# Attention's transposes as pairs of 64-row tiles, and where the early weights are converted

## The chip, the cores and the metric

One core of a Trainium2 chip runs the whole program in one launch. The metric is the device time of a run in microseconds (us); a kernel's figure is the median of its runs. TensorE is PE in the profile (PEld are its weight loads), VectorE is DVE, ScalarE is ACT, GpSimd is POOL, SyncE is SP.

## The reference, cut to what matters

```
# q, k, v: (2, 12, 448, 64); causal softmax attention, heads side by side -> x (896, 768)
scores = q k^T / 8, masked above the diagonal
attn = exp(scores - max) / (sum + 1e-9);  x = attn v
# first product pair: w_in (768, 2048), w_out (2048, 768), alpha (2048)
h = x @ w_in;  g = max(h, 0) + alpha * min(h, 0);  x = g @ w_out
# second: w1, w2, w3, w_out2, all (768, 768)
h = max(x @ w1, x @ w2, x @ w3);  out = h @ w_out2
```

## The kernel before, in words

**Products.** The weights arrive as 64-bit floats, two 32-bit words each. `Weights` turns one 128-column tile (six blocks of 128x128, 768 columns in all) into a high and a low 32-bit part, wh and wl; activations are split the same way (xh, xl or g_h, g_l). A product is three matmuls, xh wh + xl wh + xh wl (`product`, L463). Converting one tile takes these steps: a load (`raw`, L414), on ScalarE `size` (t, L426) and `low` (r, L444), on VectorE two fast operations in `high` (L430, L433), then `top` (L447) and `both` (L458, an integer addition), then wh (a cast on ScalarE, L318) and wl (a subtraction, L330).

**Attention.** There are 12 jobs, numbered 0 to 11, each a pair of heads. Keys run forwards for the first head of the pair and backwards for the second. The 448 queries form four chunks c = 0 to 3 of 64, 128, 128 and 128 rows, which see 64, 192, 320 and 448 keys. For each job:

- scores (L645) on TensorE, as pairs of 64-row matmuls, one per head, in groups of chunks (3, 0) and (2, 1); each group takes two banks of PSUM of a ring "s" of four. The 64x64 scores of chunk 0 stand first in their group;
- a masked row maximum on VectorE (L663), an exp on ScalarE (L676), one reciprocal step per group on VectorE (L688 adds eps, L689), and the normalizing of each part on GpSimd (L693), all in place in a tile e;
- 16 transposes of 128x128 on TensorE (L720, L717), four to a bank of a ring "t" of three, and four copies p of up to 512 columns out of PSUM, on ScalarE (L318) or VectorE (L324);
- the sums with v on TensorE (`pv`, L735), a cast to xh on ScalarE (L318) and xl on VectorE (L330).

**What sets the order.** All this is issued in one order per engine that a planner (`Plan`) writes before the run: of the steps that can start, it takes the one that starts earliest by its own assumed durations, and among nearly equal ones that with the lowest rank. Each engine then runs its list strictly in that order. Job i has rank 10 i plus a number per kind of step (`RANK`). Scores run two jobs ahead of the sums. `port` marks steps of VectorE that the planner keeps apart from GpSimd's.

**Early tiles.** The first three tiles of w_in (f = 0, 1, 2) are held: they are converted while attention runs, with rank 125 + 5 f - 7, and TensorE multiplies them with the first 384 tokens (the first batch) between the last jobs: 54 products of 384 columns. After attention come their 512 other tokens, then the remaining 13 tiles, then w_out, then the second pair of products. The fourth tile (f = 3) starts with a product of 384 columns.

Of the kernel before, what the change touches and what calls it, by code (L numbers as in the profile page):

```python
# [32 lines left out]
    norm=6, p=7, p_out=-4, av=6, x=15, weights=-7, prelu=-10,  # L33
# [169 lines left out]
def attention_moe_moe2_kernel(  # L203
# [25 lines left out]
    B, HP, _, _, S = qk.shape  # L229
    D = 64  # L230
    DM, NT = out.shape
    DFF = alpha.shape[0] * alpha.shape[1]
# [105 lines left out]
    class Weights:  # L338
# [3 lines left out]
        def __init__(  # L342
# [7 lines left out]
            lo_engines=("DVE", "POOL"),  # L350
            after=(),
            token="ct",
            used=None,
        ):
# [13 lines left out]
            size = plan.add(  # L368
                rank, on_act(k, words=True), partial(self.size), (load,), take=(token,)
            )  # L370
            self.size_step = size
            high = plan.add(
                rank, {"DVE": 2 * on_dve(k, fast=True)["DVE"] + 0.12}, step(self.high), (size,), port=True
            )
            low = plan.add(
                rank, on_act(k, words=True), step(self.low), (load,), take=("cr",)
            )
            top = plan.add(
                rank, on_dve(k), step(self.top), (high, low), give=(("raw", load),), port=True
            )  # L380
            both = plan.add(
                rank, on_dve(k) | on_pool(k), self.both, (top, low), give=(("cr", low),), port=True
            )
            self.whole = both
            used = used or slice(0, n)
            k = (used.stop - used.start) * P
            hi = plan.add(
                rank,
                on_act(k),
                copy(lambda: self.part(0)[:, : used.stop - used.start], lambda: f32(self.t[:, used])),  # L390
                (both,),
            )
            lo = plan.add(
                rank,
                {e: (on_dve(k) | on_pool(k))[e] for e in lo_engines},
                sub(
                    lambda: self.part(1)[:, : used.stop - used.start],
                    lambda: f32(self.t[:, used]),
                    lambda: self.part(0)[:, : used.stop - used.start],
                ),  # L400
                (hi,),
                give=((token, size),) if used.stop - used.start == n and token == "ct" else (),
                port=True,
            )
            self.ready = [lo]
# [15 lines left out]
        def size(self, engine):  # L421
            if self.token == "ct":
                self.t = wcvt.tile([P, KC, P], U32, tag="t", name="t")[:, : self.n]
            else:
                self.t = room[self.token].tile([P, KC, P], U32, tag="t", name="t")[:, : self.n]
            nc.scalar.activation(out=f32(self.t), in_=f32(self.raw[..., 1]), func=AF.Abs)  # L426

        def high(self):
            t = self.t
# [12 lines left out]
        def low(self):  # L442
            self.r = wcvt.tile([P, KC, P], U32, tag="r", name="r")[:, : self.n]
            nc.scalar.activation(out=self.r, in_=self.raw[..., 0], func=AF.Copy, scale=2.0**-29)  # L444

        def top(self):
            nc.vector.scalar_tensor_tensor(  # L447
                out=self.t,
                in0=self.raw[..., 1],
                scalar=0xC0000000,  # L450
                in1=self.t,
                op0=ALU.bitwise_and,
                op1=ALU.bitwise_or,
            )

        def both(self, engine):
            t = self.t.bitcast(I32)
            ENGINE[engine].tensor_tensor(out=t, in0=t, in1=self.r.bitcast(I32), op=ALU.add)  # L458
# [1017 lines left out]
```

## Time and profile before

| | |
|---|---|
| median of three runs | 488.33 us (488.0 to 488.43) |
| the profiled execution | 488.39 us, of which the span is 486.6 us |
| TensorE busy | 480.6 us, 99% of the span |
| VectorE, ScalarE, GpSimd busy | 384.0 (79%), 250.3 (51%), 53.7 us (11%) |
| chain that ended last, by engine | PE 88%, DVE 6%, ACT 5%, issue 1% |
| granted TensorE clock | full in all 40 slices |
| HBM | 119 GB/s over the span |

Attention lies in the first 90 us. The span is shorter than the execution, since it runs from the first to the last instruction that the profile shows. Matmuls overlap, so starts, not lengths, give TensorE's pace; on the other engines too an instruction's length includes a tail of some 0.1 us that lies beside the next one.

### The profile page before, as it was taken

How to read it: one execution, taken by the hardware profiler on the slowest of the kernel's cores; microseconds unless marked ns; L12 is line 12 of the kernel's file. 1: busy time of each engine (PE TensorE's matmuls, PEld its weight loads, DVE VectorE, ACT ScalarE, POOL GpSimd, SP SyncE). 2: the span in 40 equal slices, each digit the busy share in tenths (PEclk: the TensorE clock that was granted, in tenths of full speed). 3: DMA queues.
4: the chain of work that ended last, by engine and by line, in shares of the span. 5: the costliest groups of instructions: out<-in, count | busy, mean ns of one | idle time of the engine just before them, and what ended most of it. 6: DMA issues, size and time to landing. Idle time of an engine off the chain costs nothing.

```text
span 486.6 us, 7335 instructions
## 1 busy us (share of the span) xinstructions
PE 480.6 (99%) x2727; PEld 415.6 (85%) x2727; DVE 384.0 (79%) x750; ACT 250.3 (51%) x478; POOL 53.7 (11%) x101
## 2 busy tenths in 40 slices
PE   9999999999999999999999999999999999999997
PEld 4766668889888999898898899988899988899986
DVE  5789988589999999866647557589899999716962
ACT  5899996145535544534344425365455665305510
POOL 4557675010000000000000000000000000000000
PEclk9999999999999999999999999999999999999999
DMA  7666511113323332425233333344433554000122
GB/s 275 241 205 210 195 49 67 65 66 129 118 88 120 130 116 67 137 95 164 61 120 114 113 120 129 101 159 151 166 139 129 201 188 131 0 1 1 57 96 75
DMA packets 13859, 58.28 MB, mean 120 GB/s; under 512 B 1664, under 2 KB 3328, under 8 KB 13824
## 3 DMA queue, kind: packets, MB, share of 16 engines
q1 hardware_dynamic: 13680, 57.72, 35.5%
q8 instruction: 21, 0.34, 0.3%
q14 instruction: 14, 0.11, 0.1%
q10 hardware_dynamic: 144, 0.10, 0.1%
HBM read 55.06 MB, written 2.75 MB: 119 GB/s over the span
## 4 chain that ended last, share of the span: by engine, by line
PE 88%; DVE 6%; ACT 5%; issue 1%; POOL 0%; DVEq 0%; ACTq 0%
PE ps L463 79%; PE ps L645 3%; ACT e L676 3%; PE pv L735 3%; PE pt L720 3%; DVE xl L330 1%; DVE e L663 1%; ACT p L318 1%; PE warm L801 1%; DVE wl L330 1%; DVE t L958 1%; PE pt L717 0%; ACT xh L318 0%; DVE v L1141 0%; ACT wh L318 0%
## 5 line engine op out<-in xcount | busy, mean ns | idle before, releaser
L463 PE MATMUL ps<-xh,wl 128*128 128x384 f32 (+2 forms) x435 | 158.0, 363 | 0.0
L463 PE MATMUL ps<-xh,wh 128*128 128x384 f32 (+2 forms) x435 | 157.9, 363 | 0.0
L463 PE MATMUL ps<-xl,wh 128*128 128x384 f32 (+2 forms) x435 | 157.8, 363 | 0.0
L463 PEld LDWEIGHTS ps<-xh,wh 128*128 128x128 f32 x435 | 81.7, 188 | 8.8
L463 PEld LDWEIGHTS ps<-xl,wh 128*128 128x128 f32 x435 | 81.6, 188 | 8.7
L463 PEld LDWEIGHTS ps<-xh,wl 128*128 128x128 f32 x435 | 81.7, 188 | 8.5
L318 ACT CAST wh<-t 128x768 fp32r<-128x768 f32 (+1 forms) x52 | 42.2, 811 | 68.7 <-DVE t L458 68.5
L463 PE MATMUL ps<-g_h,wl 128*128 128x512 f32 (+1 forms) x192 | 69.7, 363 | 0.0
L463 PE MATMUL ps<-g_l,wh 128*128 128x512 f32 (+1 forms) x192 | 69.6, 363 | 0.0
L463 PE MATMUL ps<-g_h,wh 128*128 128x512 f32 (+1 forms) x192 | 69.5, 362 | 0.0
L330 DVE TENSOR_TENSOR wl<-t,wh 128x768 fp32r<-128x768 f32 (+1 forms) x48 | 44.2, 921 | 17.6 <-ACT wh L318 17.6
L458 DVE CUSTOM_DVE_ANT_0 t<-t,r 128x1536 uint16<-128x1536 uint16 (+1 forms) x58 | 53.6, 926 | 2.0
L447 DVE SCALAR_TENSOR_TENSOR t<-raw,t 128x768 uint32<-128x768 uint32 (+1 forms) x58 | 53.6, 925 | 0.9
L444 ACT ACTIVATE r<-raw 128x768 uint32<-128x768 uint32 (+1 forms) x58 | 50.9, 878 | 6.4 <-DMA raw<-in_moe_w_dram 4.5
L426 ACT ACTIVATE t<-raw 128x768 f32<-128x768 f32 (+1 forms) x58 | 51.1, 883 | 5.7 <-DMA raw<-in_moe_w_dram 3.2
L693 POOL TENSOR_SCALAR e<-e,sm 128x192 f32<-128x192 f32 (+3 forms) x84 | 43.7, 538 | 30.4 <-DVE sm L689 16.8
L676 ACT ACTIVATE e<-e,nm 128x192 f32<-128x192 f32 (+3 forms) x84 | 43.8, 526 | 5.8 <-DVE nm L663 5.6
L318 ACT CAST g_h<-g 128x384 fp32r<-128x384 f32 (+1 forms) x32 | 18.2, 568 | 49.4 <-DVE g L773 49.3
L463 PEld LDWEIGHTS ps<-g_l,wh 128*128 128x128 f32 x192 | 36.0, 188 | 3.9
L463 PEld LDWEIGHTS ps<-g_h,wh 128*128 128x128 f32 x192 | 36.1, 188 | 3.9
L463 PEld LDWEIGHTS ps<-g_h,wl 128*128 128x128 f32 x192 | 36.0, 188 | 3.8
L663 DVE CUSTOM_DVE_ANT_0 e<-ps,mask 128x192 f32<-128x192 f32 (+2 forms) x72 | 32.0, 486 | 8.8 <-PE ps L645 8.6
(95 smaller groups left out, 526.7 us busy)
## 6 DMA issues: line engine op xcount, KB each, us to landing
raw<-in_moe_w_dram SPq DMA_DIRECT2D x18, 768.0 KB, 4.3
raw<-in_moe_w_in_dram SPq DMA_DIRECT2D x16, 768.0 KB, 4.4
raw<-in_moe_w_out_dram SPq DMA_DIRECT2D x12, 768.0 KB, 4.4
raw<-in_moe_w_out_dram SPq DMA_DIRECT2D x12, 640.0 KB, 4.1
qk<-in_qk_dram SPq DMA_DIRECT2D x12, 448.0 KB, 3.6
v<-in_v_dram SPq DMA_DIRECT2D x12, 448.0 KB, 4.3
out_dram<-o SPq DMA_DIRECT2D x11, 224.0 KB, 1.9
out_dram<-o SPq DMA_DIRECT2D x1, 128.0 KB, 1.7
```

Of the source, the lines that this page charges most:

```text
L318: nc.scalar.copy(out(), src())
L330: ENGINE[engine].tensor_tensor(out=out(), in0=a(), in1=f32(b()), op=ALU.subtract)
L426: nc.scalar.activation(out=f32(self.t), in_=f32(self.raw[..., 1]), func=AF.Abs)
L444: nc.scalar.activation(out=self.r, in_=self.raw[..., 0], func=AF.Copy, scale=2.0**-29)
L447: nc.vector.scalar_tensor_tensor(out=self.t, in0=self.raw[..., 1], scalar=0xC0000000, in1=self.t, op0=ALU.bitwise_and, op1=ALU.bitwise_or,)
L458: ENGINE[engine].tensor_tensor(out=t, in0=t, in1=self.r.bitcast(I32), op=ALU.add)
L463: nc.tensor.matmul(ps, a, c, start=(first and y == 0), stop=(last and y == 2), **kw)
L645: nc.tensor.matmul(ps if c else ps[rows * j : rows * j + rows], self.qk[d, 0, START[c] : START[c] + rows], self.qk[d, 1, S - n :] if j els ...
L663: nc.vector.tensor_tensor_reduce(out=self.e_part(c, j), in0=self.ps[c, j], in1=masks[j][:, m : m + n] if c else short, op0=ALU.add, op1=AL ...
L676: nc.scalar.activation(out=s, in_=s, func=AF.Exp, scale=-1.0, bias=self.column(self.nm, i, c, j), accum_out=self.column(self.sm, i, c, j),)
L693: ENGINE[engine].tensor_scalar(out=s, in0=s, scalar1=self.column(self.sm, i, c, j), scalar2=1.0, op0=ALU.mult, op1=ALU.mult,)
L720: nc.tensor.transpose(pt[:, o : o + P], self.e[:, s : s + P], ident)
```

## The change

**Transposes.** A job's 16 transposes become 32 of 64 rows (64 rows of e, 128 columns; 64 columns out). Two that follow each other take the upper and the lower 64 rows and write different banks. They are issued in two phases of 16: the first needs only chunks 2 and 3 normalized and takes two banks of "t", the second takes one bank of "t" and a borrowed one: the next free bank of the scores' ring "s", or for the last two jobs a bank of the later products ("b"). Four copies of 512 columns bring them out, in strips of 64 columns.

**Scores.** The groups are (3), (2, 1); chunk 0 moves out of them: `first` computes it after the sums of the job two before, as a 128x64 pair (q for it comes from the host padded with zeros, so the q/k transfer grows from 448 to 480 KB). Its result lies in columns 448 to 511 of the first bank of group (3), which thus comes free only after the 64-column maximum; that bank is the one that the next second phase borrows.

**Weights of the early tiles.** Each step handles half a tile (`cuts=2`), and their rank falls from -7 to +5 beside the job's steps; wh may go to GpSimd too, and `both` and wl go to VectorE or GpSimd. `top`, `both` and one subtraction of the activations lose `port`.

**Eps.** 1e-9 is added by `tensor_tensor` with a small constant tile instead of `tensor_scalar`.

```diff
-    norm=6, p=7, p_out=-4, av=6, x=15, weights=-7, prelu=-10,
+    norm=6, p=7, p_out=-4, av=6, x=15, weights=5, prelu=-10,
...
-            self.groups = ((1, 0), (2,), (3,)) if rank == 0 else PAIRS
+            self.groups = ((1,), (2,), (3,), (0,)) if rank == 0 else ((3,), (2, 1), (0,))
+            sums = ((1,), (2,), (3, 0)) if rank == 0 else ((3,), (2, 1, 0))
...
+        def first(self, after):
+            s = self.add(
+                "s",
+                {"PE": 4 * START[1] / 2400},
+                step(self.first_scores),
+                (self.max[3, 0], *after),
+                give=(("qk", self.load),),
+                mode="columns",
+            )
+            self.soften(s, (0,), self.shared)
+            return s
...
+                        give=(("s", bank, j),) * (c == cs[-1] and (c, j) != (3, 0)),
...
+        def turn(self, after, spare):
+            self.spare = spare
             t, self.outs = None, []
-            for i, part in enumerate(PARTS):
+            for i in range(2):
+                t = self.add(
                     "p",
-                    {"PE": 4 * 0.109 + 0.02},
+                    {"PE": 8 * 0.066},
                     step(self.p_t, i),
+                    [x for (c, j), x in self.norm.items() if i or c >= 2] + (after if t is None else [t]),
+                    take=("t", spare) if i else ("t", "t", "p"),
+                    give=(("e", self.e_took),) * i,
+                    mode="rows",
                 )
...
-            nc.vector.tensor_scalar(out=sm, in0=sm, scalar1=1e-9, scalar2=None, op0=ALU.add)
+            nc.vector.tensor_tensor(out=sm, in0=sm, in1=least[:, : k[-1] + 1 - k[0]], op=ALU.add)
...
+                    for r in range(2):
+                        at_row = slice(H * r, H * r + H)
+                        nc.tensor.transpose(
+                            banks[r][:, o : o + H], self.e[at_row, s : s + P], ident[at_row, at_row]
+                        )
+                    o += H
...
-            FILL_RANK + FILL_STEP * f + RANK["weights"], w_in, 0, KC, f, lo_engines=("POOL",)
+            FILL_RANK + FILL_STEP * f + RANK["weights"], w_in, 0, KC, f, hi_engines=("ACT", "POOL",), both_engines=("DVE", "POOL",), lo_engines=("DVE", "POOL",), cuts=2
```

TensorE's order for one job in the middle of attention; before:

```order
L720 MATMUL pt<-ident,e_129 128x128 x12
L717 MATMUL pt<-ident,e_129 128x128
L720 MATMUL pt<-ident,e_129 128x128 x3
L645 MATMUL ps<-qk 64x64 x2
L645 MATMUL ps<-qk 128x448 x2
L645 MATMUL ps<-qk 128x320 x2
L645 MATMUL ps<-qk 128x192 x2
L735 MATMUL pv<-p,v 64x384 x2
```

and now (pt are transposes, ps scores, pv sums):

```order
L718 MATMUL ps<-qk 64x64 x2
L791 MATMUL pt<-ident,e_131 128x64 x32
L702 MATMUL ps<-qk 128x448 x2
L702 MATMUL ps<-qk 128x320 x2
L702 MATMUL ps<-qk 128x192 x2
L812 MATMUL pv<-p,v 64x384 x2
```

The 64x64 scores have moved ahead of the transposes, next to the sums of the job before.

VectorE's order from the last row maximum of the last job on; before:

```order
L663 ISA e_130,nm<-ps,mask_114 128x192
L663 ISA nm 128x1
L688 TENSOR_SCALAR sm_124<-sm_124 128x4
L689 RECIPROCAL sm_124<-sm_124 128x4
L324 COPY p<-pt 128x512 x2
L330 TENSOR_TENSOR xl<-pv,xh 128x448
L447 SCALAR_TENSOR_TENSOR t<-raw,t 128x768
L430 TENSOR_SCALAR t<-t 128x768
L433 TENSOR_SCALAR t<-t 128x768
```

and now (t, wl are weight steps, sm the reciprocal steps, p<-ps the copy out of the borrowed bank):

```order
L736 ISA e_132,nm<-ps,short 128x64
L736 ISA nm 128x1
L331 TENSOR_TENSOR wl<-t,wh 128x384
L331 TENSOR_TENSOR xl<-pv,xh 128x448
L325 COPY p<-ps 128x2x4x64
L467 TENSOR_SCALAR t<-t 128x384
L470 TENSOR_SCALAR t<-t 128x384
L467 TENSOR_SCALAR t<-t 128x384
L470 TENSOR_SCALAR t<-t 128x384
L487 SCALAR_TENSOR_TENSOR t<-raw,t 128x384
L761 TENSOR_TENSOR sm_124<-sm_124,least 128x6
L762 RECIPROCAL sm_124<-sm_124 128x6
```

The last part of tile 0 is converted only here, and most of tiles 1 and 2 behind it, where before only the last steps of tile 2 were left of the held ones.

GpSimd's order at the end of attention (e is normalized there); now:

```order
L766 TENSOR_SCALAR e_131<-e_131,sm_123 128x448 x2
L498 TENSOR_TENSOR t<-t,r 128x384
L321 TENSOR_SCALAR wh<-t 128x384
L766 TENSOR_SCALAR e_131<-e_131,sm_123 128x320 x2
L766 TENSOR_SCALAR e_131<-e_131,sm_123 128x192 x2
L766 TENSOR_SCALAR e_131<-e_131,sm_123 128x64
L766 TENSOR_SCALAR e_132<-e_132,sm_124 128x448 x2
L498 TENSOR_TENSOR t<-t,r 128x384
L766 TENSOR_SCALAR e_132<-e_132,sm_124 128x320 x2
L766 TENSOR_SCALAR e_132<-e_132,sm_124 128x192 x2
```

Half steps of the weights stand between the parts of the last two jobs; before, these two jobs' parts followed each other without one.

## Rows read from the trace of the kernel before

**Rows 1.** The page: busy us, share, instructions; granted clock in 40 slices.
```profile
PE 480.6 (99%) x2727; PEld 415.6 (85%) x2727; DVE 384.0 (79%) x750; ACT 250.3 (51%) x478; POOL 53.7 (11%) x101
...
PEclk9999999999999999999999999999999999999999
```

**Rows 2.** Stretch: length, busy PE, PEld, DVE, ACT, POOL, clock, DMA share, GB/s.
```profile
30.00:70.00 40.00, 39.01 (x378) 27.51 (x376) 36.70 (x141) 39.37 (x121) 27.95 (x47) 1.00 0.52 163
```

**Rows 3.** Chain of waits by line, 53.5 to 67.05 and 86.2 to 104.
```profile
by line: ACT e L676 63.6%; ACT p L318 18.6%; ACT r L444 5.9%; ACT xh L318 5.5%; ACT wh L318 5.3%; issue 1.1%; DVE nm L663 0.7%
...
by line: PE ps L463 100.3%; PE pv L735 0.3%
```

**Rows 4.** TensorE's timeline: start, length of the run, what, count.
```profile
12.19 1.53 PE L720 MATMUL pt<-ident,e 128*128 128x128 f32 x12
...
28.04 1.98 PE L735 MATMUL pv<-p,v 128*64 128x384 f32 x28
29.95 1.53 PE L720 MATMUL pt<-ident,e 128*128 128x128 f32 x12
...
32.27 2.15 PE L645 MATMUL ps<-qk 64*64 64x64 f32 x16
34.34 1.98 PE L735 MATMUL pv<-p,v 128*64 128x384 f32 x28
...
74.08 1.53 PE L720 MATMUL pt<-ident,e 128*128 128x128 f32 x12
...
103.75 0.33 PE L463 MATMUL ps<-xh,wh 128*128 128x384 f32 x1
103.92 0.34 PE L463 MATMUL ps<-xl,wh 128*128 128x384 f32 x1
```

**Rows 5.** Transposes: a run without waits; all of them, ns min/median/max (PEld: loads).
```profile
81.29 1.47 PE L720 MATMUL pt<-ident,e 128*128 128x128 f32 x12
...
L720 PEld LDWEIGHTS pt<-ident,e x180: 138/140/145, 12.2 to 82.9; 128*128 128x128 f32 x180
L720 PE MATMUL pt<-ident,e x180: 272/273/330, 12.2 to 83.0; 128*128 128x128 f32 x180
```

**Rows 6.** Weight loads of transposes and of scores, timeline of short stretches.
```profile
29.95 0.20 PEld L720 LDWEIGHTS pt<-ident,e 128*128 128x128 f32 x2
...
32.53 0.18 PEld L645 LDWEIGHTS ps<-qk 64*128 64x128 f32 x1
...
32.53 0.29 PEld L645 LDWEIGHTS ps<-qk 64*128 64x128 f32 x3
```

**Rows 7.** ScalarE: timeline around seven exps and a copy; the page's group of `size`.
```profile
9.87 0.67 ACT L676 ACTIVATE e<-e,nm 128x448 f32<-128x448 f32 x1
...
13.56 0.56 ACT L318 COPY p<-pt 128x512 f32<-128x512 f32 x1
...
69.51 0.56 ACT L318 COPY p<-pt 128x512 f32<-128x512 f32 x1
69.97 0.46 ACT L676 ACTIVATE e<-e,nm 128x192 f32<-128x192 f32 x1
...
L426 ACT ACTIVATE t<-raw 128x768 f32<-128x768 f32 (+1 forms) x58 | 51.1, 883 | 5.7 <-DMA raw<-in_moe_w_dram 3.2
```

**Rows 8.** VectorE: timeline from a job's first maximum to xl; adding eps, ns min/median/max.
```profile
71.67 0.62 DVE L663 CUSTOM_DVE_ANT_0 e<-ps,mask 128x448 f32<-128x448 f32 x1
...
74.77 1.29 DVE L324 COPY p<-pt 128x512 f32<-128x512 f32 x2
75.98 0.61 DVE L330 TENSOR_TENSOR xl<-pv,xh 128x448 fp32r<-128x448 f32 x1
...
L688 DVE TENSOR_SCALAR sm<-sm x25: 158/166/507, 8.1 to 78.4; 128x4 f32<-128x4 f32 x23, 128x2 f32<-128x2 f32 x2
```

**Rows 9.** A cast that writes strips of 128 columns, ns min/median/max.
```profile
L318 ACT CAST w1h<-t x3: 835/839/840, 327.0 to 382.0; 128x768 fp32r<-128x768 f32 x3
```

**Rows 10.** The page's DMA issues: KB each, median us from issue to landing.
```profile
qk<-in_qk_dram SPq DMA_DIRECT2D x12, 448.0 KB, 3.6
```

More of the change, by code (lines that the diff above doesn't have):

```diff
@@ L381, in __init__ @@
-            both = plan.add(
-                rank, on_dve(k) | on_pool(k), self.both, (top, low), give=(("cr", low),), port=True
-            )
+            used = used or slice(0, n)
+            whole = used.stop - used.start == n
+            ends, first, lows, highs, tops, took = [], None, [], [], [], on_act(k // cuts, words=True)
+            ks = [slice(n * i // cuts, n * (i + 1) // cuts) for i in range(cuts)]
+            m = n // cuts * P
+            for i, c in enumerate(ks):
+                size = plan.add(
+                    rank, took, step(self.size, c), (load,) if i == 0 else (load, first), take=(token,) * (i == 0)
+                )
+                if i == 0:
+                    first = size
+                highs.append(
+                    plan.add(
+                        rank,
+                        {"DVE": 2 * on_dve(m, fast=True)["DVE"] + 0.12},
+                        step(self.high, c),
+                        (size,),
+                        port=True,
+                    )
+                )
@@ new lines, in __init__ @@
+            self.size_step = first
+            for i, c in enumerate(ks):
+                low = plan.add(
+                    rank, took, step(self.low, c), (load,) if i == 0 else (load, lows[0]), take=("cr",) * (i == 0)
+                )
+                lows.append(low)
+                tops.append(
+                    plan.add(
+                        rank,
+                        on_dve(m),
+                        step(self.top, c),
+                        (highs[i], low, *tops),
+                        give=(("raw", load),) * (c is ks[-1]),
+                        )
+                )
@@ L393, in __init__ @@
[L393 to L404, printed above, removed]
@@ L416, in load, with size, high @@
             )
[L421 to L429, printed above, removed]
+        def size(self, c):
+            if c.start == 0:
+                pool = wcvt if self.token == "ct" else room[self.token]
+                self.t = pool.tile([P, KC, P], U32, tag="t", name="t")[:, : self.n]
+            nc.scalar.activation(out=f32(self.t[:, c]), in_=f32(self.raw[:, c, :, 1]), func=AF.Abs)
+        def high(self, c):
+            t = self.t[:, c]
             nc.vector.tensor_scalar(
```

309 lines of the change are left out of this document (173 added, 136 removed).

## The prediction

> **What bounds the kernel now.** I began with the page's first two parts [rows 1]: TensorE is busy for 99% of the span, the other engines for 79% at most, and its granted clock is full in all 40 slices. So TensorE's list of work sets the end, unless some stage hides a second limit behind it. The stretch from 30 to 70 us, which is all attention, does [rows 2]: ScalarE is busy for 39.37 of its 40 us, VectorE for 36.70, TensorE for 39.01. The chain of waits says the same more sharply [rows 3]: of the 13.5 us from 53.5 on, 99% lie on ScalarE: exps, copies of transposed blocks, and 11% in two weight steps (r, wh). So attention is paced by ScalarE and TensorE in turn. From 86 us on the chain is TensorE's products without a gap; what attention gives back before the product that starts at 103.75 us therefore reaches the end, if that later stage stays fed.
>
> TensorE's timeline [rows 4] gives the pace. One job is sums (28.04 to 29.95, 1.91 us), transposes (29.95 to 32.27, 2.32), scores (32.27 to 34.34, 2.07). The transposes of the first job start at 12.19 and those of the eleventh (number 10) at 74.08: ten periods, 61.9 us, 6.19 each.
>
> **TensorE's new cycle.** Removed: 16 transposes of 128x128. Twelve without a wait take 1.47 from first start to last end, one is 0.273 long, so they start (1.47 - 0.27) / 11 = 0.109 apart [rows 5]. Added: 32 transposes of 64 rows, issued as 16 pairs on the two halves of the array. No row shows such a pair. Its 64 moving columns are half of 128, so 0.055; its two weight loads still bring 128 columns each, and their price lies between two rows [rows 5, 6]. Two loads of the present transposes end 0.20 after the first starts, at 0.14 each: the second starts 0.06 after the first. Of the 64x128 loads for the scores one ends after 0.18 and three after 0.29: the load that follows a pair starts 0.11 later. So a pair costs 0.058 if its loads behave as a transpose's do, 0.109 if as the scores' do. I take 0.058, since the transpose's load is the nearer row: the same operation on the same 128 columns. That is 0.93 for a job instead of 2.32.
>
> The Trainium skill (TensorE: Matmul & The Clock Gate, LDWEIGHTS) gives a load's time as its columns over 1.2, whatever the rows: 107 ns for 128 columns, by which halving the rows wins nothing and the sum would be the first rival's. The 0.11 of the scores' loads agrees with it, the 0.06 of the transposes' loads doesn't.
>
> The 64x64 scores leave the middle of the score group and become a 128x64 pair next to the sums. The rest of the group begins at 32.53 [rows 6] and lasts 1.81; the pair is two passes of 64 columns, 0.11. Sum: 1.91 + 0.11 + 0.93 + 1.81 = 4.76 us, against 6.19.
>
> **ScalarE and VectorE.** Seven exps in a row run from 9.87 to 13.56, 3.69; a copy of 512 columns from 69.51 to 69.97, 0.46 [rows 7]; the cast xh has 448, so 0.41. The new order gives ScalarE 23 copies over some 11 jobs, 0.96 a job, and 8 half steps of weights before its last exps, at half of 0.883: 3.5 over ten jobs, 0.35. Sum 5.41. VectorE [rows 8]: seven maxima and one reciprocal step 3.10 (71.67 to 74.77), a second step 0.3, two copies 1.21 (74.77 to 75.98), xl 0.53 (448 of 512), seven half steps of weights about 0.25: 5.4 at most, for a job with two copies. So the pace passes to ScalarE, and the transposes alone would not have bought it: of its 39.37 us in that stretch, 6.09 a period, what goes away is mostly weight work, which now ranks behind the jobs.
>
> I take **5.5 a period**: 5.41, and the 0.1 a job that ScalarE idles even now (0.63 us in 40). The bounds: 5.2 if VectorE takes a copy more where it has room and nothing else waits; 6.0 if the new waits for banks add up (second rival). TensorE then reaches the transposes of job 10 at 12.2 + 10 x 5.5 = 67.2, against 74.08: **6.9 us**.
>
> **The end of attention.** From there to 103.75 it is 29.67 now. In the new order TensorE has two sets of transposes (1.9), two of sums (3.8), 54 products of 384 columns (9.3, at 0.173, from 103.75 to 103.92 [rows 4]) and 54 of 512 (12.4, at four thirds of it): 27.4. The weights now come late, so I counted VectorE's new order after its last maximum, which ends some 0.6 after those transposes start. Up to w1's last half: six half steps at 0.47, one at 0.53, four fast ones at 0.3, xl twice, a copy, a reciprocal: 2.8 + 0.5 + 1.2 + 1.1 + 0.6 + 0.3 = 6.5, at 7.1. Up to w2's last half 8.1 more, at 15.2. TensorE needs w1's last half at about 11 and w2's at 16 to 17, since it now does the first tile's late 512 columns before w2's early ones. So the late weights cost nothing, with 1 to 2 us to spare; if that cover is gone, each us missing is a wait. GpSimd's half step of w1 stands ahead of five normalizing steps of job 11, which the last transposes await: about 0.3; the bank for job 10's second transposes comes free only with the last maximum: 0.3; latencies 0.3. So 28.3, a gain of **1.4 us**.
>
> **The small parts.** Adding eps with two tensors frees VectorE from waits of up to 0.51 where 0.166 is normal [rows 8], under 1 us in all, on an engine that does not pace: nothing. The copies grow from 1856 to 2048 columns a job, which the counts above hold, and write strips of 64; a cast of 768 that writes strips of 128 elements takes 0.839 [rows 9], and half steps of plain rows 0.44: strips are free. The q/k transfer grows from 448 to 480 KB; it is issued a job ahead, but the first stands before the first scores: a fourteenth of its 3.6 us [rows 10], 0.26, at most, nothing at least; I take 0.1. After 103.75 TensorE's order is unchanged, and by the same count the next weights are ready some 8 us before their use: nothing lost.
>
> **Sum.** 6.9 + 1.4 - 0.1 = 8.2 us. The profiled execution took 488.39 with a span of 486.6; the median of the three runs is 488.33, so the same 1.8 lie around the span. 488.3 - 8.2 = **480.1 us**.
>
> **Rivals.**
> 1. *The pairs don't run at 0.058:* the halves take turns, or load as the scores do. Then 0.109 a pair: cycle 4.76 + 16 x 0.05 = 5.56, with 0.3 of bank waits 5.9; 12.2 + 59 = 71.2, a gain of 2.9, and the two sets at the end lose 1.6 against the 1.4 won there: 2.6, **485.7**. For it: the 0.11. Against: the 0.06. Chance 0.09.
> 2. *The borrowed bank becomes the wait.* The second transposes need a bank of the scores that comes free only after the 64-column maximum, the last of VectorE's seven, and the 320-column scores then need that bank back, after its copy. Ahead of this copy in VectorE's order stand xl (0.53) and another copy (0.6); with its own 0.6 and 0.2 of latency that is 1.9, less the 0.75 of the 448-column scores: 1.2 a job, and 0.2 for the maximum. In full it makes 4.76 + 1.4 = 6.2; ScalarE can take the copy, so I price it at 6.0: 1.9 + 1.0 - 0.1 = 2.8, **485.5**. For it: copies p already stand on the chain, 18.6% of that stretch [rows 3]. Against: the new order gives more copies to ScalarE than to VectorE, 23 against 20 in that stretch. Chance 0.12.
> 3. *Slower: the clock falls.* With TensorE busy for 4.8 of 5.5 us, the granted clock could fall to the lower level, 1.2 GHz, in attention. A job then takes 2 x 4.76 = 9.5, 3.3 more than now, while each other one gains 0.7; from three such jobs of ten on the gain is gone (9.9 - 4.8 - 1.4 = 3.7, **492**), with ten it is 32 slower. Against it: full clock in all slices, with transposes a third of the time (2.32 of 6.19) and holes at the start [rows 1, 4]. Chance 0.05. [...]
> 4. *No change:* each engine runs its order blindly, and with three nearly equal engines every mismatch of the assumed durations becomes a wait. Periods stay at 6.19 and the end gives nothing: **488**. Chance 0.03.
>
> The forecast keeps 0.71. Its own span is from 5.2 a period (3 less, 477.1) to 5.75 (482.6). The range goes a little below that for a smoother end, and above it to rivals 1 and 2 but for their worst: 476.7 to 485.3. A measurement of this kernel tells about 0.2%, 1 us, from no change. Faster by more: 0.71 + 0.09 + 0.12 = 0.92; within it, rival 4, 0.03; slower, 0.05.
>
> **What would show it.** Pairs of transposes about 0.058 apart, sixteen in 0.93 to 1.2 us; periods of 5.4 to 5.6; job 10's transposes near 67 us, the fourth tile's first product of 384 columns near 95.5; ScalarE over 95% busy from 20 to 65, TensorE at 85 to 90% there, clock full, and no holes after. Wrong: pairs at 0.1; a period near 6; holes in TensorE ahead of the 320-column scores or of the early products.

## The result, and the profile after

The changed kernel takes **482.26 us** (median of four runs, 481.88 to 482.68) against 488.16 (487.63 to 488.43, four runs) of the kernel before on the same chip: a ratio of 0.9882, with a 95% interval of 0.9866 to 0.9898. That is 5.9 us faster, inside the range that was given and 2.2 us above the predicted 480.1. The profiled execution took 482.68 us, its span is 480.9.

The page of the changed kernel: busy us, share of the span, instructions; the granted clock in 40 slices; the chain that ended last by engine.

```profile
PE 473.1 (98%) x2919; PEld 410.6 (85%) x2919; DVE 389.8 (81%) x764; ACT 250.3 (52%) x481; POOL 62.3 (13%) x109
...
PEclk9999999999999999999999999999999999999999
...
PE 87%; DVE 9%; POOL 2%; issue 1%; ACT 0%; DVEq 0%; POOLq 0%
```

Beside [rows 1], TensorE has lost 7.5 us of its time, and ScalarE's total has not moved. The chain has changed hands: before, 5% of it lay on ScalarE and 6% on VectorE; now ScalarE has none and VectorE 9%.

TensorE's timeline of the changed kernel around its landmarks (start, length of the run, what, count, and in brackets what it waited for): job 1's and job 5's transposes, the end of attention from job 10's transposes on, and the fourth tile's first product.

```profile
16.92 1.34 PE L791 MATMUL pt<-ident,e 64*128 64x64 f32 x32
...
38.35 0.96 PE L791 MATMUL pt<-ident,e 64*128 64x64 f32 x16
...
68.08 0.71 PE L791 MATMUL pt<-ident,e 64*128 64x64 f32 x16
...
68.84 0.22 PE L791 MATMUL ps<-ident,e 64*128 64x64 f32 x1
68.87 0.22 PE L791 MATMUL pt<-ident,e 64*128 64x64 f32 x1
68.90 0.22 PE L791 MATMUL ps<-ident,e 64*128 64x64 f32 x1
...
69.33 0.45 PE L503 MATMUL ps<-xh,wh 128*128 128x384 f32 x1
69.61 0.34 PE L503 MATMUL ps<-xl,wh 128*128 128x384 f32 x1
...
70.86 0.34 PE L503 MATMUL ps<-xh,wl 128*128 128x384 f32 x1
71.12 1.98 PE L812 MATMUL pv<-p,v 128*64 128x384 f32 x28
...
74.80 0.71 PE L791 MATMUL pt<-ident,e 64*128 64x64 f32 x16
75.81 0.27 PE L791 MATMUL ps<-ident,e 64*128 64x64 f32 x1 [0.30 <-POOL e L766]
...
76.67 0.44 PE L503 MATMUL ps<-xh,wh 128*128 128x384 f32 x1
...
97.69 0.33 PE L503 MATMUL ps<-xh,wh 128*128 128x384 f32 x1
```

Two landmarks settle where the time came from. Job 10's transposes start at 68.08 where they started at 74.08 [rows 4]: **6.0 us from attention**. From there to the fourth tile's product at 97.69 it is 29.61 us, where it was 29.67: **nothing from the end of attention**. Behind that the two kernels run in step; the products are 6.06 us earlier up to 454 us. (In the last 24 us this one execution's products follow at 0.207 instead of 0.203 us and give back 0.35. Of the kernels below, which share that order, four show 0.203 and eight 0.207; what decides it was not found.)

The stretches of the changed kernel: length, busy PE, PEld, DVE, ACT, POOL, clock, DMA share, GB/s. The first answers to [rows 2]; the others are jobs 1 to 4 and jobs 5 to 9.

```profile
30.00:70.00 40.00, 38.37 (x532) 27.86 (x531) 38.44 (x154) 38.92 (x125) 27.70 (x53) 1.00 0.43 145
...
16.92:38.35 21.43, 21.40 (x308) 15.74 (x304) 19.98 (x83) 20.91 (x69) 12.54 (x27) 1.00 0.73 253
38.35:68.08 29.73, 28.11 (x381) 19.93 (x382) 28.74 (x115) 28.78 (x94) 21.84 (x42) 1.00 0.42 140
```

Nine periods from 16.92 to 68.08 make 5.68 us each: the first four 21.43 / 4 = 5.36, the last five 29.73 / 5 = 5.95. In the first four ScalarE is the fullest by its rows (20.91 of 21.43). TensorE counts as busy for 21.40 there, and the chain of waits over these four jobs lies on it:

```profile
by line: PE ps L702 37.2%; PE pv L812 35.8%; PE pt L791 24.5%; PE ps L718 2.2%; POOL e L766 1.8%; issue 0.2%
```

But a matmul's length covers short waits around it: job 1's scores take 2.19 us (18.09 to 20.28), those of job 4 take 1.89 (34.35 to 36.24). Which of the two engines sets the 5.36 is not shown. In the last five, where six of the eight half steps on ScalarE up to there lie, VectorE (28.74) and ScalarE (28.78) are both 97% busy. The chain of waits from 40 to 61 us, by line:

```profile
by line: DVE e L736 38.2%; DVE p L325 16.3%; issue 14.8%; DVE sm L761 8.0%; DVE xl L331 7.6%; PE pt L791 3.3%; DVE t L487 2.7%; DVE t L467 2.7%; DVE t L498 2.2%; DVE sm L762 2.0%; DVE nm L736 1.9%; DVEq L736 0.4%; DVE t L470 0.3%
```

Some 82% of it lies on VectorE: maxima (e), copies (p), the addition of eps (sm, 8%), xl and weight steps; 15% is issue and 3% TensorE. In [rows 3], over 53.5 to 67.05 us of the kernel before, the same view was 99% ScalarE.

### The profile page after: what moved, and what is told of

It reads as the page before. It is cut to its first block, busy times and chain, and to the rows that moved or that the text cites. A ratio compares the mean times of both kernels' runs of the same rounds, so it can differ in the third digit from the quotient of the medians.

```text
span 480.9 us, 7762 instructions
## 1 busy us (share of the span) xinstructions
PE 473.1 (98%) x2919; PEld 410.6 (85%) x2919; DVE 389.8 (81%) x764; ACT 250.3 (52%) x481; POOL 62.3 (13%) x109
## 4 chain that ended last, share of the span: by engine, by line
PE 87%; DVE 9%; POOL 2%; issue 1%; ACT 0%; DVEq 0%; POOLq 0%
PE ps L503 79%; PE ps L702 3%; PE pv L812 2%; DVE e L736 2%; DVE xl L331 2%; PE pt L791 2%; POOL e L766 1%; DVE p L325 1%; PE warm L877 1%; DVE wl L331 1%; DVE t L1039 1%; DVE sm L761 0%; DVE v L1222 0%; DVE t L467 0%; DVE t L487 0%
## 5 line engine op out<-in xcount | busy, mean ns | idle before, releaser
L319 ACT CAST wh<-t 128x768 fp32r<-128x768 f32 (+2 forms) x53 | 41.8, 788 | 66.3 <-DVE t L498 59.2
L331 DVE TENSOR_TENSOR wl<-t,wh 128x768 fp32r<-128x768 f32 (+2 forms) x54 | 49.6, 919 | 17.1 <-ACT wh L319 17.1
L463 ACT ACTIVATE t<-raw 128x768 f32<-128x768 f32 (+2 forms) x61 | 51.9, 851 | 16.1 <-DMA raw<-in_moe_w_dram 10.3
L487 DVE SCALAR_TENSOR_TENSOR t<-raw,t 128x768 uint32<-128x768 uint32 (+2 forms) x61 | 56.5, 928 | 0.8
L482 ACT ACTIVATE r<-raw 128x768 uint32<-128x768 uint32 (+2 forms) x61 | 51.8, 849 | 2.4 <-DMA raw<-in_moe_w_dram 1.4
L498 DVE CUSTOM_DVE_ANT_0 t<-t,r 128x1536 uint16<-128x1536 uint16 (+2 forms) x53 | 48.3, 912 | 2.3
L766 POOL TENSOR_SCALAR e<-e,sm 128x192 f32<-128x192 f32 (+3 forms) x84 | 42.7, 529 | 23.7 <-DVE sm L762 12.7
L498 POOL TENSOR_TENSOR t<-t,r 128x384 int32<-128x384 int32 (+1 forms) x8 | 13.3, 1665 | 243.7 <-PE ps L503 201.0
```

The costliest lines, as they stand in the source:

```text
L319: nc.scalar.copy(out(), src())
L331: ENGINE[engine].tensor_tensor(out=out(), in0=a(), in1=f32(b()), op=ALU.subtract)
L463: nc.scalar.activation(out=f32(self.t[:, c]), in_=f32(self.raw[:, c, :, 1]), func=AF.Abs)
L482: nc.scalar.activation(out=self.r[:, c], in_=self.raw[:, c, :, 0], func=AF.Copy, scale=2.0**-29)
L487: nc.vector.scalar_tensor_tensor(out=self.t[:, c], in0=self.raw[:, c, :, 1], scalar=0xC0000000, in1=self.t[:, c], op0=ALU.bitwise_and, op1 ...
L498: ENGINE[engine].tensor_tensor(out=t, in0=t, in1=self.r[:, c].bitcast(I32), op=ALU.add)
```

## The experiments

Each kernel was compared with the kernel before on the same chip, whose median was 488.4 us each time (488.2 beside the changed kernel), so a few tenths between rows of the table mean nothing. The landmarks are TensorE's in the profiled execution: the mean of nine periods (jobs 1 to 10), job 10's transposes (T10), and from there to the fourth tile's first product of 384 columns (end).

| kernel | us | ratio to before (95%) | period | T10 | end |
|---|---|---|---|---|---|
| before | 488.2 | 1 | 6.27 | 74.08 | 29.67 |
| changed | 482.26 | 0.9882 (0.9866 to 0.9898) | 5.68 | 68.08 | 29.61 |
| old transposes | 489.81 | 1.0037 (1.0025 to 1.0049) | 6.47 | 75.19 | 29.97 |
| old weights | 488.49 | 1.0001 (0.9991 to 1.0011) | 5.98 | 70.11 | 33.28 |
| early rank | 483.29 | 0.9912 (0.9896 to 0.9928) | 5.68 | 68.03 | 32.33 |
| whole steps | 486.41 | 0.9963 (0.9951 to 0.9976) | 5.79 | 68.33 | 32.71 |
| eps by tensor_scalar | 482.44 | 0.9881 (0.9867 to 0.9896) | 5.73 | 68.08 | 29.62 |
| unpaired | 483.25 | 0.9896 (0.9881 to 0.9911) | 5.75 | 68.76 | 30.00 |
| no borrowed bank | 486.42 | 0.9962 (0.9949 to 0.9974) | 6.06 | 71.08 | 30.99 |
| the same, unpaired | 486.76 | 0.9962 (0.9948 to 0.9976) | 5.98 | 69.79 | 31.14 |
| half copies | 479.09 | 0.9812 (0.9799 to 0.9826) | 5.41 | 65.19 | 29.47 |
| no eps | 481.06 | 0.9852 (0.9839 to 0.9866) | 5.58 | 66.65 | 29.75 |
| no eps, GpSimd without two-tensor steps | 481.50 | 0.9860 (0.9847 to 0.9874) | 5.65 | 67.40 | 29.11 |
| no eps, replanned | 480.76 | 0.9853 (0.9837 to 0.9870) | 5.58 | 65.90 | 30.00 |

### The two halves of the change, one at a time

**Old transposes, new weights.** The kernel before with the changed `Weights` class, rank and eps:

```diff
-    norm=6, p=7, p_out=-4, av=6, x=15, weights=-7, prelu=-10,
+    norm=6, p=7, p_out=-4, av=6, x=15, weights=5, prelu=-10,
...
-FILL_RANK + FILL_STEP * f + RANK["weights"], w_in, 0, KC, f, lo_engines=("POOL",)
+FILL_RANK + FILL_STEP * f + RANK["weights"], w_in, 0, KC, f, hi_engines=("ACT", "POOL",), both_engines=("DVE", "POOL",), lo_engines=("DVE", "POOL",), cuts=2
```

> The kernel before with only the weights' part and eps of the change: half steps, rank +5, wider choice of engines; transposes of 128 rows, groups (3, 0) and (2, 1), no borrowed bank. Theory W (the one of the prediction: the gain is mostly weight work that leaves attention, the transposes alone would not have bought it): most of the 5.9 us comes here, 483 to 485 us. Theory E (VectorE and ScalarE share their work out and together pace attention; TensorE's old cycle, some 5.8 us without waits, is the next limit at once): 486 us (485 to 487.2), periods near 6.0. Theory T (TensorE's shorter cycle is all): no gain, 488 (487.5 to 488.7).

Measured: 489.81, slower than before by 1.4. No theory had that. The periods grew from 6.27 to 6.47. Two of the longest pieces of its chain between 40 and 62 us (start, us, what) are GpSimd's normalizing:

```profile
45.19 2.24 POOL e L735 x3
48.38 2.15 POOL e L735 x4
```

That is 4.4 of the 22 us. In this kernel's order GpSimd has eleven half steps of weights among its normalizing, where the changed kernel has five. That they make the 1.4 us was not tried apart.

**New transposes, old weights.** The changed kernel with the class, the rank and the engines of before (the two lines above the other way round).

> The changed kernel with the weights' part of before: whole steps, rank -7, wh on ScalarE and wl of the held tiles on GpSimd alone. Up to the last exp its order has 7 whole weight steps on ScalarE where the changed kernel has 8 halves (1.7 us more), and some 2 us more on VectorE. Theory E: the two engines share that, so attention is 1.9 us longer, and up to 0.5 of it comes back behind, as tile 0 is ready earlier: 483.9 us (483.2 to 485). Theory W: most of the gain is lost, 486 to 488. Theory T: 482.3, as the changed kernel, within 0.5.

Measured: 488.49, the same as before. So the two parts bring +1.4 and 0.1 us alone and -5.9 together. Theory W comes nearest by value (486 to 488), but the table shows that its place is wrong: the period falls to 5.98 and job 10's transposes come 4.0 us earlier than before. Of that, 3.6 are lost again in the 33.28 us behind them. The place inside attention differs too. Mean periods of jobs 1 to 4 and of jobs 5 to 9 are 6.18 and 6.34 before, 6.23 and 6.67 with the new weights alone, 5.36 and 6.47 with the new transposes alone, 5.36 and 5.95 with both. So in jobs 1 to 4, where ScalarE has one whole step of weights in this kernel and two halves in the changed one, the new transposes bring the whole gain by themselves; only in jobs 5 to 9 does it take both parts.

**Where old weights lose it: rank, or whole steps?** Two kernels take them apart: the changed kernel with `weights=-7`, and the changed kernel with `cuts=1`.

> The changed kernel with rank -7 for the held weights, halves and engines as changed. The planner takes what starts earliest and asks for the rank only among near equals; up to the last exp its order has 9 half steps on ScalarE against 8, and one wl, one both and one xl more on VectorE against two copies that go the other way. Theory E: attention 0.5 to 1 us longer, the end 0.3 shorter: 482.6 us (482.0 to 483.3). Theory W: the ranking carries the gain, 485 or more.

> The changed kernel with the held weights in whole steps (one cut), its rank and its choice of engines as changed. Between the changed kernel (482.3) and the one with the old weights' part (488.5) lie the rank, worth 1.0 by its own run, the halves and GpSimd's share. Theory H: the length of a step is what matters; a whole step of 0.8 to 0.95 us (two in a row in high) stands in VectorE's list ahead of maxima and copies that TensorE waits for: 487 us (485.5 to 488.5), periods of 6.2 to 7 from job 6 on, and the last maximum 1 us or more later. Theory G: GpSimd's part of the conversion is what matters: 483 us (482.3 to 484).

Measured: 483.29 and 486.41. By time, theories E and H have it. By place, E has not: job 10's transposes come at 68.03, as in the changed kernel, and not 0.5 to 1 us later. H has it in part: the last maximum comes 2.2 us later and two periods reach 7.0 and 6.9, but the later ones make that up and job 10's transposes come at 68.33. Both kernels lose behind them. TensorE's timeline of the early-rank kernel there, then the last maximum on VectorE in that kernel and in the changed one:

```profile
68.03 0.71 PE L791 MATMUL pt<-ident,e 64*128 64x64 f32 x16
70.82 0.34 PE L791 MATMUL ps<-ident,e 64*128 64x64 f32 x1 [2.08 <-DVE nm L736]
...
70.45 0.22 DVE L736 CUSTOM_DVE_ANT_0 e<-ps,short 128x64 f32<-128x64 f32 x1
...
68.32 0.22 DVE L736 CUSTOM_DVE_ANT_0 e<-ps,short 128x64 f32<-128x64 f32 x1
```

And the stretches behind it (columns as above; the third number from the end is the granted clock):

```profile
70.00:71.00 1.00, 0.18 (x4) 0.21 (x6) 0.64 (x7) 1.00 (x6) 0.54 (x1) 0.91 0.00 0
71.00:72.00 1.00, 1.00 (x17) 0.88 (x16) 0.05 (x1) 0.78 (x5) 0.71 (x2) 0.50 0.00 0
72.00:74.00 2.00, 2.00 (x6) 1.65 (x6) 1.90 (x6) 2.00 (x5) 0.90 (x2) 0.50 0.03 8
...
76.00:78.00 2.00, 2.00 (x40) 1.63 (x35) 1.66 (x4) 1.12 (x2) 0.00 (x0) 1.00 0.00 0
```

Job 10's second transposes wait 2.08 us for their borrowed bank, which the last row maximum (nm) frees. In this kernel's list VectorE does a `both`, a wl, a copy and an xl ahead of its last maxima, which are done only at 70.6; in the changed kernel they are done at 68.5. And after that hole TensorE runs at the lower level, 1.2 GHz (0.50), for some 3 us. The clock does not fall in every execution: over this kernel's six, two had a mean clock of 0.996 and took 485.0 and 485.4, four had 1.000 and took 483.0 to 483.3. So the late maximum costs 1 us, and the fall of the clock 2 more when it comes. The old-weights kernel has the same hole and the fall in ten of its eleven executions (488.0 to 489.1); the one without it took 486.26, 2.1 below the kernel before. So of the 6.2 us between old weights and the changed kernel some 2 go with the clock. The whole-steps kernel waits at the same place, and its clock falls too in the profiled execution; its five times (486.1 to 486.9) do not split that way. The two holes, old weights first:

```profile
72.67 0.34 PE L752 MATMUL ps<-ident,e 64*128 64x64 f32 x1 [1.84 <-DVE nm L697]
...
70.89 0.24 PE L791 MATMUL ps<-ident,e 64*128 64x64 f32 x1 [1.86 <-DVE nm L736]
```

VectorE's timeline in the whole-steps kernel shows what whole steps do to a job, and TensorE's the scores beside them:

```profile
45.96 0.95 DVE L487 SCALAR_TENSOR_TENSOR t<-raw,t 128x768 uint32<-128x768 uint32 x1
46.83 0.68 DVE L325 COPY p<-pt 128x512 f32<-128x512 f32 x1
47.43 0.95 DVE L498 CUSTOM_DVE_ANT_0 t<-t,r 128x1536 uint16<-128x1536 uint16 x1
48.30 0.51 DVE L761 TENSOR_TENSOR sm<-sm,least 128x6 f32<-128x6 f32 x1
```

```profile
47.57 1.13 PE L702 MATMUL ps<-qk 64*128 64x320 f32 x6 [0.60 <-DVE p L325]
```

One whole step stands ahead of the copy out of the borrowed bank, which the scores at 47.57 await, the other ahead of the next job's maxima. This job's period is 6.97 us, where the changed kernel's is 5.32; others are shorter, so that by job 10 little of it is left.

### What the new transposes bring

**Without the pairs.** The transposes of a phase in another order, all of the upper rows first:

```diff
-            for g, blocks in enumerate(PLACES):
-                for k, block in enumerate(blocks[PHASES[i]]):
...
-                    for r in range(2):
...
+            for r in range(2):
...
+                for g, blocks in enumerate(PLACES):
+                    for k, block in enumerate(blocks[PHASES[i]]):
```

> The changed kernel with the 16 transposes of a phase in another order on TensorE: first all eight of the upper 64 rows, then all eight of the lower, so that neighbours use the same half of the array and the same bank. If the halves of a pair run beside each other only when they alternate, a transpose costs 0.055 (half of the old 0.109) and a job 1.76 instead of 0.98 us: 0.78 more for each of 12 jobs where TensorE paces, about half of it where VectorE and ScalarE do (from 38 to 68 us): +6 us, 488 (485.5 to 491). If a transpose of 64 rows is 0.03 in any order: 482.3, the same within 0.5.

Measured: 483.25, 1.0 more by the medians (no run of one kernel reaches those of the other); by the ratios to before it is 0.7, with intervals that overlap. The traces side with the 1.0: job 10's transposes come 0.7 later and the end is 0.4 longer. The transposes do run as the first theory says. The same 16 in this kernel's timeline, beside 68.08 above:

```profile
68.76 1.01 PE L790 MATMUL pt<-ident,e 64*128 64x64 f32 x16
```

That is (1.01 - 0.24) / 15 = 0.051 apart, against (0.71 - 0.24) / 15 = 0.031 in pairs (0.24 is the length of one). But these 32 x 0.02 = 0.6 us a job moved the periods from 5.68 to 5.75 only. TensorE has most of that as room in every job: of the 6 us that the first theory expected, 5 were hidden. The unpaired order also writes eight transposes in a row to one bank; whether the half of the array or the bank makes the 0.051 was not tried.

**Without the borrowed bank.**

```diff
-                    take=("t", spare) if i else ("t", "t", "p"),
+                    take=("t", "t") if i else ("t", "t", "p"),
...
-                            give=(("t", t, k) if i == 0 else ("t" if k else spare, t),),
+                            give=(("t", t, k),),
...
-            banks = [ps_t.tile([P, BANK], F32, tag="t", name="pt") for _ in range(2 - i)]
-            if i:
-                banks.insert(0, ps_s.tile([P, BANK], F32, tag="s", name="pt") if self.spare == "s" else bank())
+            banks = [ps_t.tile([P, BANK], F32, tag="t", name="pt") for _ in range(2)]
```

> The changed kernel whose second phase of transposes takes two banks of the ring of three, as the kernel before did for its fourth bank, and borrows none; pairs, moved first scores and half steps as changed; the order is planned anew under that rule. The pairs themselves were worth only 1.0 us (unpaired), so something else in the new transposes brings what the half steps alone don't (489.8 with the old transposes). Theory B: it is the bank; the second phase again waits for a copy of the first, some 0.4 a job, in all jobs: 486.5 us (485 to 488.5). Theory P: it is the two phases and the moved first scores, which let TensorE start before all parts are normalized: 483 us (482.3 to 484.2).

> The same without the borrowed bank, and with each phase's transposes in the unpaired order, so that TensorE's time for them is that of the kernel before (1.76 against 1.74 us a job). Theory B: with the copy's wait in TensorE's path, the 0.8 us a job is no longer hidden: 489 us (487.5 to 490.5), near the 489.8 of the old transposes with half steps. Theory P: 484 us (483.2 to 485.5).

Measured: 486.42 and 486.76. Theory B holds for the first: the bank, with the lists planned anew without it, is worth 4.2 us. TensorE's waits in that kernel (for what: us in all, times, longest):

```profile
PE pt L789 <- ACT p L319: 6.7, 10, 0.9
PE pt L789 <- POOL e L766: 1.9, 5, 0.7
```

Ten of the twelve jobs wait for a copy on ScalarE, up to 0.9 us. For the second kernel theory B is wrong: with the copy in the way it makes no difference that can be told whether the transposes before it are paired. And 3.0 us still lie between it and the old transposes with half steps, though TensorE's time for the transposes is nearly the same in both. They must be in what else differs (two phases, the moved first scores, copies of 512, the lists that follow from them); that was not taken apart.

### What paces attention

**Half of each copy left out, and eps left out.** The lists of all engines stay as they are in both. The first kernel leaves out half of the transposed blocks and so does not compute the whole result; the second leaves out the addition.

```diff
-                            copy(partial(self.p_part, i, k), partial(self.pt.get, (i, k))),
+                            copy(partial(self.p_part, i, k), lambda i=i, k=k: self.pt[i, k][:, :1]),
...
-            return p[:, :, PHASES[i], r]
+            return p[:, :1, PHASES[i], r]
...
-                        self.p[:, at_col[j] : at_col[j] + end - q],
+                        self.p[:, at_col[j] % 1024 : at_col[j] % 1024 + end - q],
```

```diff
-            nc.vector.tensor_tensor(out=sm, in0=sm, in1=least[:, : k[-1] + 1 - k[0]], op=ALU.add)
```

> The changed kernel with half of each copy out of PSUM left out (256 columns instead of 512; the sums read the copied half twice, so half of the transposed blocks is left out of the result); the order of all engines as it is. It frees VectorE of 0.53 and ScalarE of 0.43 us a job, at the same number of instructions. Theory E (the two engines pace attention from 38 to 68 us): five periods fall from 5.95 to some 5.4, the earlier ones lose only their waits for the borrowed bank: job 10's transposes at 64.5, 478.5 us (477 to 480). Rival (the pace is a chain through GpSimd's normalizing or TensorE itself): 481.5 or more.

> The changed kernel without the addition of eps (each sum holds the 1 of its own maximum, beside which 1e-9 vanishes in 32 bits); the order of all engines as it is. VectorE loses 24 instructions which take 0.1 to 0.2 us of its time each, and one 0.94. Theory E: 0.3 a job, where VectorE paces (five jobs), and less in the others: 480.8 us (480.2 to 481.8). Rival (VectorE does not pace): 482.3 within 0.4.

Measured: 479.09 and 481.06, both as theory E has it: work taken from VectorE, or from VectorE and ScalarE, comes off the time, though TensorE's list is the same to the row. The periods come to 5.41 and 5.58. Both rule out TensorE as what sets the pace. The half copies also rule out the chain through GpSimd: TensorE's recorded waits for normalizing between job 1's and job 10's transposes stay at 1.5 us, and the periods of jobs 5 to 9 still become 0.35 shorter. The kernel without eps could not rule it out by itself: there GpSimd gets its sums earlier too, and those waits shrink to 0.7. Half copies also free banks earlier, but the 1.1 us that TensorE's weight loads wait for copies in all nine periods (the row under rival 2 below) are less than the 2.4 that these periods give back. In jobs 1 to 4 leaving out eps changes nothing (5.34 against 5.36), and half copies give 0.17: there VectorE does not set the pace.

**Which addition of eps.**

> The changed kernel with eps added by tensor_scalar again; the order of all engines stays as it is. The changed kernel's two-tensor addition takes 0.16 us, but up to 0.94 where GpSimd runs an operation of two tensors. If the stretch comes from GpSimd's two-tensor work against any second input of VectorE, tensor_scalar is shorter there and VectorE, which paces late attention, wins up to 1 us: 481.3 to 482. If tensor_scalar waits for GpSimd as much or more (0.51 at most in the kernel before), the time stays or rises: 482.3 to 484. My value: 482.3, no difference over 0.5.

Measured: 482.44, the same, as the value given there. Where VectorE's addition is stretched, the kind of addition makes no difference. All 25 in the kernel with tensor_scalar, and all 25 in the changed one (ns min/median/max):

```profile
L758 DVE TENSOR_SCALAR sm<-sm x25: 164/169/950, 6.7 to 71.9; 128x2 f32<-128x2 f32 x13, 128x6 f32<-128x6 f32 x11, 128x4 f32<-128x4 f32 x1
```

```profile
L761 DVE TENSOR_TENSOR sm<-sm,least x25: 154/161/942, 7.1 to 71.9; 128x2 f32<-128x2 f32 x13, 128x6 f32<-128x6 f32 x11, 128x4 f32<-128x4 f32 x1
```

### Faster versions

> The kernel without eps (481.1), the planner told so (0.2 us for a reciprocal step), and the two-tensor half steps of the held weights (both, wl) kept on VectorE, so that GpSimd, where one takes 1.0 us, does not place them ahead of its normalizing; wh may still go there. Theory N (GpSimd's half steps delay job 11's normalizing, and with it the last transposes, by 0.6 us, and stretch VectorE's work): 480.3 us (479.6 to 480.8). Rival: VectorE, which paces, takes the 0.5 us of each of these steps itself and attention grows by 1: 481.1 to 482.2.

The edit on the kernel without eps: `both_engines=("DVE",), lo_engines=("DVE",)` for the held weights, and 0.2 for the reciprocal step in the planner. Measured: 481.50, 0.4 above the kernel without eps: the rival by value. Both halves of the dispute can be seen in the table. The end falls by 0.64 us to 29.11, which is theory N's 0.6, but job 10's transposes come 0.75 later; VectorE does these steps now, though that this is the reason was not tried apart. The two nearly cancel: the fourth tile's product comes 0.11 later. The rest of the 0.4 lies in the last 24 us, where this trace has the pace of 0.207 and the one without eps 0.203.

> The kernel without eps (481.1), with the planner told that a reciprocal step takes 0.2 us and with the row maxima's rank lowered from 12 to 9, which lets them go ahead of the reciprocal steps and of some copies; all engines as in the changed kernel. The work is the same, only its order differs. If VectorE and ScalarE are as full as the traces say (28 to 29 of 30 us each), an order can only remove what they idle: 480.7 us (480.0 to 481.6), the fastest of all kernels by a little or none. Rival: later reciprocal steps hold up GpSimd's normalizing, for which TensorE waits: 481.6 to 483.

The edit: `max=9` in `RANK`, and the same 0.2. Measured: 480.76 (480.49 to 482.10), not to be told from 481.06. The kernel without eps is the fastest of these that computes the whole, by 1.2 us against the changed one; leaving out the addition alters nothing there, since each sum holds the 1 of its own maximum.

## Why the prediction was right, and what was mis-sized

**The sign held, and its reason in part.** The prediction had attention paced by ScalarE and TensorE in turn, and said that the transposes alone would not have bought the gain. Old weights with new transposes are at 488.49, old transposes with new weights at 489.81: lifting one limit alone lowered no median. But the new transposes alone buy all of the gain in jobs 1 to 4, and 2.1 us of the total in the one execution in which the clock did not fall. The reason given for the weights' half was not right. "What goes away is mostly weight work, which now ranks behind the jobs": up to its last exp ScalarE does ten whole steps of weights before (8.9 us), 8.1 us of them with the new weights alone, seven whole steps with the new transposes alone (6.3), six whole ones with whole steps (5.4), nine halves with the early rank (4.9) and eight halves in the changed kernel (4.4). So more of that work goes with the new transposes than with the new weights, the halves take 1.0 us of it, and the rank 0.5.

**Attention, forecast 6.9, measured 6.0.** The sum started at the first job's transposes and took ten periods of 5.5. Two errors in it partly cancel, so that it is so near is in part luck: the periods over jobs 1 to 9 are 5.68, nine times 0.18 or 1.7 us too long in all, and job 1's transposes come at 16.92, 0.8 earlier than the 17.7 of the sum. For jobs 1 to 4 ScalarE's 5.41 and its 0.1 of idle are near (5.36, of which it is busy for 5.23). The term that was mis-sized is VectorE's "5.4 at most": it does 28.74 / 5 = 5.75 us a job in jobs 5 to 9, as the weight steps lie there and not evenly over ten jobs, and as additions of eps were stretched. ScalarE's half steps too lie six to two.

**TensorE's cycle.** The pair at 0.058 was nearly right: 2 x 0.031. What was wrong is what it was taken for. The 2.32 us that transposes took before were read as 16 transposes to be removed. At 0.109 these make 1.74; the rest is waits, in the job read there for a copy:

```profile
31.68 0.33 PE L717 MATMUL pt<-ident,e 128*128 128x128 f32 x1 [0.20 <-ACT p L318]
```

The pairs themselves are worth 0.7 to 1.0 us of the total, the bank without which the second phase waits for a copy 4.2. Rival 1, which put pairs at 0.109, was priced at 485.7; the unpaired kernel is that rival made real, and it takes 483.25. Its pair of 0.109 is near the measured 2 x 0.051, but the price was laid on a path that TensorE does not set.

The Trainium skill (TensorE: Matmul & The Clock Gate, LDWEIGHTS) gave a load of 128 columns 107 ns; here a load takes 0.138 us (the median of all the transposes' loads), yet two of them start every 0.063, so that by the trace the rule is no floor for their pace. The Trainium skill (TensorEngine Tiling (Array Packing), Key Properties) says that different tiles can load weights and multiply in parallel; 0.031 against 0.051 agrees with it, as far as the bank is not the reason.

**Rival 2, the borrowed bank.** The wait that it describes is there. The scores' weight loads in the changed kernel, from 16.92 to 68.08 (what, for what: us in all, times, longest):

```profile
PEld ps L702 <- DVE p L325: 1.1, 5, 0.3
```

That is 1.1 us over nine periods, in five waits, against 1.2 a job in its pricing. The bank gives 4.2.

**The end of attention, forecast 1.4, measured 0.06.** The counted parts are right one by one: sums 2 x 1.91, 512-column products 12.4, and no product waits for a weight, as forecast. Two terms fail. The 54 products of 384 columns were priced at 0.173 each, 9.3; they take 10.26, because they come in five stretches, and each change of kind costs about 0.1 on either side (why is not shown): in the rows above 0.28 from 69.33 to 69.61, and 0.26 from 70.86 to 71.12, where 0.173 is the pace. [Rows 4] start at 103.75, in the middle of a long stretch, and could not show that. And two sets of transposes take 3.12 (68.08 to 69.33, 74.80 to 76.67), where 1.9 and 0.9 of allowances were set down: job 11's second phase starts at 75.81, held by GpSimd, which has a half step (`both`) ahead of its normalizing:

```profile
72.02 1.01 POOL L498 TENSOR_TENSOR t<-t,r 128x384 int32<-128x384 int32 x1 [1.89 <-DVE sm L761]
73.02 3.03 POOL L766 TENSOR_SCALAR e<-e,sm 128x320 f32<-128x320 f32 x5
```

The same count for the old end would have shown the first error: 2 x 1.74 + 3.8 + 9.3 + 12.4 = 29.0, against the 29.67 that it took.

**Rival 3, the clock.** It did not happen in the changed kernel, whose clock is full in all slices and whose TensorE waits 0.5 us at the longest once attention is under way. But it happens in three neighbours of it, in one place, after a hole of 1.8 to 2.1 us. In two of them it costs about 2 us, not 4 to 32: the prediction had it come from TensorE's short idle in every job, and here it comes behind one long hole.

**The small parts.** Eps by two tensors: nothing, as said, but not for the reason given. It frees VectorE from no wait (0.942 us at the longest, against 0.950 with one tensor), and on VectorE, which does pace late attention, such a wait counts. The larger q/k transfer: 0.1 was set down; the first scores start at 4.22 us before and after, so it is nothing. Behind 103.75 nothing was lost but the 0.35 in the last 24 us of the profiled execution.

**The signs that were named.** Pairs 0.06 apart: seen. Periods of 5.4 to 5.6, job 10 near 67, the fourth tile near 95.5: they came to 5.68, 68.08 and 97.69. ScalarE over 95% busy: 97% from 30 to 70, but over jobs 5 to 9 VectorE is as full. No holes behind attention: seen. TensorE's share was a bad sign: at 38.37 of 40 us it looks as full as before, since ends of matmuls are modelled and a matmul's length covers the short waits around it; that most of a job's 0.6 us could be added to its work unseen shows how much room such a share hides.

## What to carry to other kernels

Where two engines stand at nearly the same pace, test the parts of a change in pairs: each half alone can show nothing in the total, or less, and both together everything; then look at the stretches, where one half may have gained what another place lost. An interval in a timeline is not the price of the instructions in it; divide it into pace and wait, at both ends of each stretch, before removing it. In a list that runs strictly in order, the length of the filler steps matters as much as their sum, most of all just ahead of an instruction that frees a bank.

## What the runs showed that was not expected

**VectorE's small additions wait for GpSimd.** In the changed kernel and in the one with old weights, an addition of 2 or 6 columns is as long as the rest of GpSimd's instruction beside it. First the changed kernel, then the other (VectorE's row and GpSimd's):

```profile
53.68 0.94 DVE L761 TENSOR_TENSOR sm<-sm,least 128x6 f32<-128x6 f32 x1
...
53.60 1.00 POOL L331 TENSOR_TENSOR wl<-t,wh 128x384 fp32r<-128x384 f32 x1
```

```profile
57.52 1.60 DVE L722 TENSOR_TENSOR sm<-sm,least 128x2 f32<-128x2 f32 x1
...
57.28 1.82 POOL L331 TENSOR_TENSOR wl<-t,wh 128x768 fp32r<-128x768 f32 x1
```

They end at 54.62 and 59.12, each 0.02 after GpSimd's 54.60 and 59.10; twice the step on GpSimd, nearly twice the wait on VectorE. The Trainium skill (SBUF — State Buffer, Who interferes with whom) has the port that the two share as an exclusive lock; the trace agrees, for additions with one tensor as for those with two. So a long GpSimd step can cost VectorE too.

**The fall of the clock is not in every execution** of the same kernel (early rank: two of six; old weights: ten of eleven), so that each of these two kernels has two times, some 2 us apart. The third kernel with such a hole, whole steps, shows no such split.
